# The last quarter of a seven-product matmul: one product moved to the end, cut into two column halves, and its last sums on VectorE

## The chip, the cores and the metric

One core of one Trainium2 chip runs the whole kernel. The metric is device time in microseconds (us), the median of several executions. Engines: TensorE (PE), VectorE (DVE), ScalarE (ACT), GpSimd (POOL) and SyncE (SP), which here only issues DMAs and waits.

## The reference, cut to what matters

```python
# x [8, 8, 512, 64], state [8, 8, 32, 64]; w_in [512, 2048], w_out [2048, 512]
a      = softmax(x @ state^T / 8)          # tokens read the states
xread  = a @ state
a2     = softmax(state @ x^T / 8)          # states read the tokens
sread  = a2 @ x
x      = concat([xread, sread], axis=2)    # 544 rows a batch, heads side by side: 4352 x 512
h      = x @ w_in
g      = max(h, 0) + alpha * min(h, 0)
out    = g @ w_out                         # float32, 4352 x 512
```

## The kernel before

**Blocks.** The 4352 rows are worked as nine blocks: block `b` from 0 to 7 holds the 512 token rows of batch `b`, block 8 all 256 state rows. In a block, `F` makes one of sixteen tiles of h (128 of the 2048 inner columns by all rows) in PSUM, `N` takes its negative part on ACT, `G` adds it back, scaled, on DVE: that is g, in float16. Four tiles of g make a group; `g_half(b, th, f)` is one half `th` of the rows of group `f`.

**The second matmul in seven products.** For blocks 1 to 8, g (row halves by inner halves) times w_out (inner halves by column halves) is done as a two-by-two product in seven products instead of eight. The sums of w_out that this needs are made once (`W`). The sums of g are made for each block: token `U.b.i.c.e` makes sum `i` (1 to 4) of inner quarter `c` on engine `e` (`p` is GpSimd, `v` VectorE); sum 2 needs sum 1, and sum 4 needs sum 2. Token `P.b.p.i.c` is product `p`, row part `i` of a half (two of them, in block 8 only one), inner quarter `c`: four matmuls of 256 columns that use four tiles of g, or of a sum, as weights (products 1, 2 and 4 use g itself, 5 sum 1, 6 sum 2, 7 sum 3, 3 sum 4). Line 736 is the one matmul of all products.

**Three accumulators.** In each block, PSUM bank x takes products 1, 6, 5 and 3 one after the other; after 1, after 6 and after 5 its content is copied aside by ACT (`K.b.1`, `K.b.2`, `K.b.4`, line 752). Bank y takes product 2 alone, bank v first 7 and then 4. Token `Q.b.th.dh` writes a quarter (row half `th`, column half `dh`) of the block: `Q.b.0.0` is y plus copy 1, `Q.b.1.1` is v after product 7 plus copy 4, `Q.b.1.0` is v after product 4 plus copy 2 (DVE, line 769), `Q.b.0.1` is x as it is after product 3 (a copy, line 767). SP then stores the quarter (line 770): 256 KB in blocks 1 to 7, 128 KB in block 8. So `Q.b.1.1` has to read v before product 4 is added to it, and each copy of x has to be done before the next product is added.

**Order and buffers.** The order is written out: a list of tokens, worked from left to right. Each engine's instructions stand in the order of the list, and an instruction waits until what it reads has been written, and until the buffer that it writes has been read by all that read the tile in it before. The buffers that matter here:

```python
osb = moe.tile([128, n_i, d_h], F32, name=f"oq_{b}_{th}_{dh}", tag="osb", bufs=4)
t = gss[b, i, c] = moe.tile(
    [128, 4, w], F16, name=f"gsum_{b}_{i}_{c}", tag=f"gsum{i}{c}", bufs=1
)
```

A quarter to be stored lies in one of four `osb` buffers and frees it when its store has landed; each sum of g has one buffer for all blocks, and frees it when the last matmul of its product is done. The list before ends (`g` of block 8 is done at its start):

```
G.8.9 P.7.5.1.0 U.8.3.0.p P.7.2.1.1 P.7.5.0.0 P.7.7.0.1 Q.7.0.0 P.7.7.1.1 P.8.2.0.1.1 K.7.4.a P.7.3.1.1 P.7.3.0.1
U.8.1.1.p U.8.2.1.p P.8.1.0.0.3 U.8.1.0.p U.8.2.0.p Q.7.1.1 P.7.4.0.1 P.7.4.1.0 P.8.1.0.1 K.8.1.a U.8.4.1.p P.7.4.0.0
P.7.4.1.1 Q.7.1.0 P.8.6.0.1 P.8.6.0.0 P.7.3.1.0 P.8.2.0.0 P.7.3.0.0 K.8.2.a P.8.5.0.1 U.8.3.1.p Q.8.0.0 P.8.5.0.0
K.8.4.a P.8.7.0.0.4 P.8.7.0.1 Q.7.0.1.v P.8.3.0.1 U.8.4.0.p Q.8.1.1 P.8.3.0.0 P.8.4.0.1 Q.8.0.1.a P.8.4.0.0 Q.8.1.0
```

At the very end SP waits, one after the other, for the semaphores of the DMAs and the engines (line 816), and then all engines meet in a barrier.

Of the kernel before, what the change touches and what calls it, by code (L numbers as in the profile page):

```python
# [8 lines left out]
F32 = mybir.dt.float32  # L9
# [29 lines left out]
tt.2 F.2.15.2 F.2.1.0 P.1.2.0.0 P.1.1.0.0 F.2.14.5 m.3.1 N.2.15 N.2.1 G.2.15 K.1.1.a N.2.14 mo.3.1.a G.2.1 G.2.14
m.3.0.1.2 mo.3.0.v.1 P.1.2.1.0 F.2.11.0 U.1.3.1.p mo.3.0.a.0 U.1.2.1.p P.1.6.1.1 N.2.11 F.2.2.5 N.2.2 F.2.0.2 N.2.0  # L40
U.1.1.0.p U.1.2.0.p U.1.4.0.p lx.4 P.1.6.0.1 Q.1.0.0 G.2.11 m.5.0.1.4 mo.5.0.a.0 G.2.2 mo.5.0.a.1 rd.2.0 rdo.2.a
G.2.0 sc.3 m.3.3.5.1 mo.3.3.a.1 tm.3 mo.3.3.v.0 m.4.0.4.2 mo.4.0.a.1 sb.3 P.1.6.1.0 P.1.6.0.0 xd.4 F.2.13.0 F.2.7.1
mo.4.0.a.0 F.2.8.2 K.1.2.a P.1.5.1.0 N.2.7 nb.3.a G.2.7 N.2.13 G.2.13 N.2.8 G.2.8 F.2.9.5 N.2.9 G.2.9 te.3.0
P.1.5.0.0 smax.3 P.1.7.1.1.4 F.2.10.1 N.2.10 F.2.5.0 N.2.5 G.2.5 G.2.10 F.2.4.2 N.2.4 G.2.4 te.3.1 P.1.5.1.1
U.1.3.0.p P.1.7.1.0 P.1.5.0.1 K.1.4.a U.1.4.1.p F.2.3.5 N.2.3 G.2.3 P.1.7.0.1 F.2.6.0 N.2.6 ssh.p.3 lx.5 F.2.12.1
N.2.12 G.2.6 P.1.7.0.0 P.1.3.1.0 m.6.0 Q.1.1.1 m.4.1.2.5 sexp.3 P.1.3.1.1 mo.6.0.a G.2.12 mo.4.1.a.0 ssum.3.0
U.2.1.0.p snorm.v.3 P.1.3.0.0 P.1.4.0.0 mo.4.1.a.1 P.1.3.0.1 U.2.2.0.p Q.1.0.1.a P.1.4.1.1 tsum.3 m.6.1.1.2 wb.3
mo.6.1.a.0 m.4.3 mo.4.3.a m.5.3.5.3 P.1.4.0.1 mo.5.3.a.1 P.2.1.0.1.1 P.2.1.1.0 P.1.4.1.0 mo.5.3.a.0 sc.4 U.2.1.1.p
U.2.2.1.p Q.1.1.0 U.2.4.1.p tn.3.0.p U.2.3.0.p U.2.3.1.p tm.4 mo.6.1.a.1 m.4.2.0.3 mo.4.2.a.0 F.3.15.5 xd.5 N.3.15
G.3.15 F.3.1.2 F.3.8.4 N.3.1 G.3.1 N.3.8 mo.4.2.a.1 P.2.1.0.0 F.3.12.0 N.3.12 G.3.8 nb.4.a P.2.1.1.1 F.3.7.5 G.3.12  # L50
# [52 lines left out]
def kernel(  # L103
# [38 lines left out]
    def single(k, name, shape, dtype):  # L142
        return ps.tile(shape, dtype, name=name, tag=f"k{k}", bufs=1)
# [584 lines left out]
    def product(b, p, i, c, k=None):  # L728
# [6 lines left out]
        for j in range(4):  # L735
# [85 lines left out]
```

## Time and profile before

| what | value |
|---|---|
| device time, median of 3 runs | 209.06 us (209.02, 209.06, 209.43) |
| span of the profiled execution, first to last instruction | 207.1 us |
| TensorE busy | 200.4 us, 97% of the span |
| GpSimd busy | 179.5 us, 87% |
| VectorE busy | 171.7 us, 83% |
| ScalarE busy | 155.3 us, 75% |
| moved by DMA | 23.68 MB, mean 114 GB/s |
| granted TensorE clock, mean | 0.996 |

Of the profiled execution only the span is given as its own time; the median of the runs is 2.0 us above that span, which is what lies around the first and the last instruction. Engine times are sums of busy time, and an engine that waits is not busy. The views give starts in us from the start of the span. A matmul's duration holds its way through the array, so several overlap: the pace of a stream of matmuls is read from the starts of neighbouring groups.

### The profile page before, as it was taken

The page shows a single profiled execution, that of the slowest core. Times are in us where ns is not written, and L with a number is a line of the kernel's source. Part 1 is how long each engine was busy: PE and PEld are TensorE (multiplying, and loading weights), DVE is VectorE, ACT ScalarE, POOL GpSimd, SP SyncE. Part 2 cuts the span into 40 slices and gives each one's busy share as a digit, 9 for nine tenths or more (in the row PEclk, how much of TensorE's full clock was granted, in tenths as well). Part 3 has the DMA queues.
Part 4 walks back from the last instruction along what each step waited for, and adds up shares of the span by engine and source line. Part 5 has one row for each costly group of instructions (what it writes and reads, how often), then busy time and mean ns, then how long its engine had stood idle before and what let it go on. Part 6 is the DMA issues. An engine that isn't in the chain of part 4 may idle for free.

```text
span 207.1 us, 5034 instructions
## 1 busy us (share of the span) xinstructions
PE 200.4 (97%) x1997; PEld 133.6 (65%) x1997; DVE 171.7 (83%) x251; ACT 155.3 (75%) x306; POOL 179.5 (87%) x113
## 2 busy tenths in 40 slices
PE   7899999999999999999999999999999999999992
PEld 2553344445566656687667856776877687788882
DVE  0889899999999999999999999999987967733231
ACT  4699999998999999997899787968755757502120
POOL 8177789997998999997997999797997999999960
PEclk9999999999999999999999999999999999999998
DMA  6999996698928798238976530126101200023223
GB/s 175 215 207 205 204 204 97 158 173 106 178 82 101 116 192 156 53 38 167 243 118 104 148 105 0 54 103 152 55 0 53 102 0 3 0 101 104 101 77 125
DMA packets 44038, 23.68 MB, mean 114 GB/s; under 512 B 22256, under 2 KB 43504, under 8 KB 44016
## 3 DMA queue, kind: packets, MB, share of 16 engines
q1 hardware_dynamic: 31152, 14.82, 28.4%
q0 software_dynamic: 11792, 8.09, 27.3%
q10 hardware_dynamic: 1072, 0.46, 0.9%
q8 instruction: 15, 0.25, 0.4%
q14 instruction: 7, 0.06, 0.1%
HBM read 17.31 MB, written 8.91 MB: 127 GB/s over the span
## 4 chain that ended last, share of the span: by engine, by line
PE 86%; DVE 5%; ACT 4%; DMA 2%; issue 1%; ACTq 0%
PE px L736 26%; PE h L577 24%; PE pv L736 13%; PE py L736 7%; PE m_ps L528 4%; PE h L586 3%; PE o L647 3%; DVE g L633 3%; DMA x<-in_x_dram 2%; PE sr_ps L501 2%; PE fill L253 2%; ACT neg L630 1%; PE sc L335 1%; ACT m L554 1%; PE xT_ps L320 1%
## 5 line engine op out<-in xcount | busy, mean ns | idle before, releaser
L633 DVE SCALAR_TENSOR_TENSOR g<-neg,oma_sb,h 128x512 f16<-128x512 f32 (+1 forms) x142 | 94.0, 711 | 11.6 <-ACT neg L630 11.0
L630 ACT ACTIVATE neg<-h 128x512 f32<-128x512 f32 (+1 forms) x142 | 75.6, 580 | 16.5 <-PE h L577 11.5
L577 PE MATMUL h<-aT,m 128*128 128x512 f16 x252 | 66.8, 380 | 0.1
L736 PEld LDWEIGHTS <-gsum 128*128 128x128 f16 x480 | 46.5, 98 | 13.1 <-issue 0.9
L736 PEld LDWEIGHTS <-g 128*128 128x128 f16 x360 | 34.7, 98 | 8.8 <-issue 1.4
L715 POOL TENSOR_TENSOR gsum<-g,g 128x1024 f16<-128x1024 f16 (+1 forms) x16 | 32.1, 2007 | 6.7 <-DVE g L633 4.9
L577 PEld LDWEIGHTS <-m 128*128 128x128 f16 x252 | 23.8, 98 | 18.4 <-issue 2.0
L715 POOL TENSOR_TENSOR gsum<-g,gsum 128x1024 f16<-128x1024 f16 (+1 forms) x16 | 32.0, 2005 | 1.5 <-PE px L736 1.0
L715 POOL TENSOR_TENSOR gsum<-gsum,g 128x1024 f16<-128x1024 f16 (+1 forms) x16 | 32.1, 2007 | 1.0
L736 PE MATMUL px<-ws,gsum 128*128 128x256 f16 x240 | 32.1, 273 | 0.0
L715 POOL TENSOR_TENSOR gsum<-g 128x1024 f16<-128x1024 f16 (+1 forms) x16 | 31.9, 2006 | 0.0
L752 ACT COPY kept<-px 128x512 f32<-128x512 f32 (+1 forms) x24 | 13.6, 567 | 21.0 <-PE px L736 20.9
L554 ACT CAST m<-m_ps 128x512 f16<-128x512 f32 x35 | 19.1, 602 | 1.5 <-PE m_ps L528 1.1
L769 DVE TENSOR_TENSOR oq<-pv,kept 128x512 f32<-128x512 f32 (+1 forms) x16 | 10.4, 649 | 10.6 <-PE pv L736 10.4
L736 PE MATMUL px<-w_out_sb,gsum 128*128 128x256 f16 x120 | 17.2, 273 | 0.0
L736 PE MATMUL px<-w_out_sb,g 128*128 128x256 f16 x120 | 17.2, 273 | 0.0
L405 POOL TENSOR_TENSOR ts<-ts,mx 128x1024 f32<-128x1024 f32 x7 | 13.3, 1911 | 4.4 <-DVE mx L400 4.4
L647 PE MATMUL o<-w_out_sb,g 128*128 128x512 f16 x64 | 16.6, 380 | 0.1
L736 PE MATMUL py<-w_out_sb,g 128*128 128x256 f16 x120 | 16.6, 273 | 0.0
L736 PE MATMUL pv<-ws,gsum 128*128 128x256 f16 x120 | 16.4, 273 | 0.0
L736 PE MATMUL pv<-ws,g 128*128 128x256 f16 x120 | 15.9, 273 | 0.0
L552 ACT CAST m<-m_ps 128x1024 f16<-128x1024 f32 x13 | 13.2, 1018 | 0.5 <-PE m_ps L528 0.4
(75 smaller groups left out, 238.1 us busy)
## 6 DMA issues: line engine op xcount, KB each, us to landing
out_dram<-oq SPq DMA_DIRECT2D x28, 256.0 KB, 2.6
xg<-in_x_dram POOLq DMA_DIRECT2D x7, 512.0 KB, 7.4
w_in_sb<-in_moe_w_in_dram POOLq DMA_DIRECT2D x4, 512.0 KB, 8.6
w_out_sb<-in_moe_w_out_dram POOLq DMA_DIRECT2D x4, 512.0 KB, 12.7
out_dram<-osb SPq DMA_DIRECT2D x4, 256.0 KB, 2.9
x<-in_x_dram SPq DMA_DIRECT2D x2, 256.0 KB, 3.7
out_dram<-oq SPq DMA_DIRECT2D x4, 128.0 KB, 2.1
x<-in_x_dram ACTq DMA_DIRECT2D x1, 256.0 KB, 4.6
```

Source lines behind the costliest of these rows:

```text
L405: engine(e).tensor_tensor(blocks(cols(live["ts", b], j, S)), blocks(scored(b, j)), over_blocks(cols(live["mx", b], j, S // N)), ALU.subtract,)
L528: nc.tensor.matmul(t[N * k : N * (k + 1), :], st_head(b, h)[64 * r : 64 * r + 64, :], w_in_sb[64 * r : 64 * r + 64, c, 512 * f : 512 * (f ...
L552: copier(e)(m_tile(b, f), t)
L554: copier(e)(m_tile(b, f)[:, g, :], t[g])
L577: nc.tensor.matmul(h.rearrange("p (r j s) -> p r j s", r=2, j=2), ms[b, f][:, g, 128 * j : 128 * (j + 1)], weights(b, g), start=(g == 0), ...
L630: nc.scalar.activation(neg, h, RELU, bias=0.0, scale=-1.0)
L633: nc.vector.scalar_tensor_tensor(g_tile(b, jc), negs.pop((b, jc)), oma_sb[:, jc : jc + 1], hs.pop((b, jc)), ALU.mult, ALU.add,)
L647: nc.tensor.matmul(outs[b, q], g_tile(b, jc)[:, 128 * q : 128 * (q + 1)], w_out_sb[:, jc, :], start=not begun and jc == 2 * jc2, stop=left ...
L715: engine(e).tensor_tensor(t, x(), y(), op)
L736: nc.tensor.matmul(pbanks[b, name][:, i, :], of(b, c)[:, j, 128 * i : 128 * (i + 1)], moving[:, 4 * c + j, :], start=not begun and j == 0, ...
L752: copier(e)(t, pbanks[b, "x"])
L769: nc.vector.tensor_tensor(osb, pbanks[b, name], kept[b, add], ALU.add)
```

## The change

- Product 2 of block 8 (`P.8.2.0.1` and `P.8.2.0.0`, eight matmuls of 256 columns) and `Q.8.0.0` are taken out of the middle of the list. In their place, at its end, `L.0` and `L.1` make the same product in two column halves of 128, each in a bank of its own (eight matmuls of 128 columns each), and `LO.0` and `LO.1` add copy 1 (DVE) and store 64 KB each, the first through ACT's queue, the second through SP's.
- Seven of the eight sums of g of block 8 are made on VectorE (`U.8.x.x.v`) and stand earlier in the list; `U.8.3.0` stays on GpSimd.
- `Q.7.0.1` stands a little earlier.
- The stores of `Q.3.1.1`, `Q.4.0.0` and `Q.4.1.1` are issued as two DMAs of 128 KB each.

```diff
 G.8.9 P.7.5.1.0 U.8.3.0.p P.7.2.1.1 P.7.5.0.0
+U.8.1.1.v U.8.2.1.v
 P.7.7.0.1 Q.7.0.0 P.7.7.1.1
-P.8.2.0.1.1
 K.7.4.a
+U.8.1.0.v U.8.2.0.v
 P.7.3.1.1 P.7.3.0.1
-U.8.1.1.p U.8.2.1.p
 P.8.1.0.0.3
-U.8.1.0.p U.8.2.0.p
 Q.7.1.1 P.7.4.0.1 P.7.4.1.0
+U.8.4.1.v U.8.3.1.v U.8.4.0.v
 P.8.1.0.1 K.8.1.a
-U.8.4.1.p
 P.7.4.0.0 P.7.4.1.1 Q.7.1.0 P.8.6.0.1 P.8.6.0.0 P.7.3.1.0
-P.8.2.0.0
 P.7.3.0.0 K.8.2.a P.8.5.0.1
-U.8.3.1.p Q.8.0.0
+Q.7.0.1.v
 P.8.5.0.0 K.8.4.a P.8.7.0.0.4 P.8.7.0.1
-Q.7.0.1.v
 P.8.3.0.1
-U.8.4.0.p
 Q.8.1.1 P.8.3.0.0 P.8.4.0.1 Q.8.0.1.a P.8.4.0.0
+L.0.1
 Q.8.1.0
+LO.0 L.1.0 LO.1
...
+    def last_part(n, k):
+        part = slice(d_h // 2 * n, d_h // 2 * (n + 1))
+        t = pbanks[B, "y", n] = single(k, f"py_{B}_{n}", [128, d_h // 2], F32)
+        for jc in range(n_h):
+            c, j = divmod(jc, 4)
+            nc.tensor.matmul(
+                t, g_half(B, 0, 2 + c)[:, j, :], w_halves[1, 0][:, jc, part],
+                start=(jc == 0), stop=(jc == n_h - 1),
+            )
+
+    def last_part_out(n):
+        part = slice(d_h // 2 * n, d_h // 2 * (n + 1))
+        osb = moe.tile([128, d_h // 2], F32, name=f"oq_{B}_0_0_{n}", tag="osb", bufs=4)
+        nc.vector.tensor_tensor(osb, pbanks[B, "y", n], kept[B, 1][:, 0, part], ALU.add)
+        (nc.sync if n else nc.scalar).dma_start(quarter_rows(B, 0, 0)[:, :, part], osb)
...
-        nc.sync.dma_start(quarter_rows(b, th, dh), osb if b < B else osb[:, 0, :])
+        to = quarter_rows(b, th, dh)
+        if b < B and e == 2:
+            for i in range(n_i):
+                nc.sync.dma_start(to[:, i, :], osb[:, i, :])
+        else:
+            nc.sync.dma_start(to, osb if b < B else osb[:, 0, :])
...
-        "W": w_sum, "U": g_sum, "P": product, "K": keep, "Q": quarter_out,
+        "W": w_sum, "U": g_sum, "P": product, "L": last_part, "LO": last_part_out, "K": keep, "Q": quarter_out,
```

(`Q.3.1.1`, `Q.4.0.0` and `Q.4.1.1` get a last argument of 2, which is `e` in the code above.)

More of the change, by code (lines that the diff above doesn't have):

```diff
@@ L96 @@
-K.8.1.a U.8.4.1.p P.7.4.0.0 P.7.4.1.1 Q.7.1.0 P.8.6.0.1 P.8.6.0.0 P.7.3.1.0 P.8.2.0.0 P.7.3.0.0 K.8.2.a P.8.5.0.1
-U.8.3.1.p Q.8.0.0 P.8.5.0.0 K.8.4.a P.8.7.0.0.4 P.8.7.0.1 Q.7.0.1.v P.8.3.0.1 U.8.4.0.p Q.8.1.1 P.8.3.0.0 P.8.4.0.1
-Q.8.0.1.a P.8.4.0.0 Q.8.1.0
+W.1.0.p G.0.6 S.0.1.0 m.1.1 F.0.10.1 N.0.4 G.0.4 mo.1.1.a N.0.10 G.0.10 F.0.8.3 S.0.1.3 S.0.1.2 ssh.p.1 sexp.1 F.0.9.0
+ssum.1.s N.0.9 lx.2 xd.2 S.0.0.3 N.0.8 G.0.8 F.0.11.1 N.0.11 S.0.3.3 W.1.1.p snorm.p.1 m.0.3 mo.0.3.a S.0.3.2 S.0.0.2
@@ new lines @@
+P.2.2.0.0 tsum.4 P.2.2.0.1 U.2.4.0.p lx.6 P.2.7.1.1 tm.5 P.2.7.0.1 F.3.5.2 F.3.13.4 sexp.4 G.3.10 nb.5.a te.5.0
+U.3.1.0.p U.3.2.0.p N.3.5 tn.4.0.a ssum.4.3 P.2.7.0.0 P.2.3.1.1 Q.2.1.1 P.2.2.1.1 snorm.v.4 P.2.3.0.1 te.5.1 G.3.5
+P.2.3.0.0 P.2.4.0.0 P.2.4.1.1 tsum.5 tn.4.1.a P.2.3.1.0 N.3.13 tn.5.1.a tn.5.0.a tt.5 wb.4 G.3.13 P.2.4.0.1
+P.3.1.0.0.3 P.2.4.1.0 Q.2.1.0 Q.2.0.1.a P.3.1.0.1 F.4.3.2 Q.2.0.0 F.4.7.4 N.4.3 F.4.11.1 U.3.1.1.p F.4.5.0 N.4.7
+P.3.1.1.1 G.4.3 F.4.10.5 G.4.7 N.4.11 G.4.11 F.4.9.2 F.4.12.4 P.3.1.1.0 F.4.8.1 N.4.5 G.4.5 N.4.10 G.4.10 U.3.2.1.p
@@ new lines @@
+N.4.9 G.4.9 F.4.2.0 K.3.1.a U.3.4.1.p N.4.12 G.4.12 P.3.6.0.0 N.4.8 F.4.13.5 G.4.8 N.4.2 G.4.2 P.3.6.1.0 N.4.13
+P.3.6.0.1 m.7.0.2.4 mo.7.0.a.0 mo.7.0.a.1 sb.5 rd.5.1 rdo.5.a tt.4 rd.4.0 rdo.4.a xd.6 G.4.13 F.4.14.2 N.4.14
+P.3.6.1.1 F.4.15.4 K.3.2.a sc.6 G.4.14 m.6.3.1.0 tm.6 m.7.3.5.2 N.4.15 P.3.5.1.1 G.4.15 mo.7.3.a.0 mo.7.3.a.1
+U.3.3.0.p mo.6.3.a.1 P.3.5.1.0 F.4.6.5 N.4.6 F.4.4.2 N.4.4 sb.6 G.4.4 P.3.5.0.1 smax.5 lx.7 P.3.5.0.0 P.3.7.0.0.4
+K.3.4.a nb.6.a te.6.0 F.4.0.0 N.4.0 U.3.3.1.p F.4.1.2 N.4.1 mo.6.3.a.0 P.3.3.0.1 te.6.1 P.3.7.1.0 U.3.4.0.p P.3.7.1.1
@@ new lines @@
+P.6.7.1.0 F.7.1.0 N.7.1 F.8.5.4 N.8.5 G.7.1 F.7.10.2 U.7.2.1.p N.7.10 G.7.10 P.6.5.0.0 K.6.4.a P.6.2.0.0.1 G.8.5
+F.7.9.0 P.6.2.1.1 P.7.1.0.1.2 P.7.1.0.0 N.7.9 P.6.2.0.1 G.7.9 P.6.2.1.0 P.6.7.0.0 F.8.9.4 P.6.3.0.1 P.7.2.0.0.0
+P.6.3.0.0 U.7.1.0.p Q.6.1.1 P.7.1.1.1 P.6.4.0.0 P.6.4.0.1 P.6.4.1.0 Q.6.0.0 P.6.4.1.1 Q.6.1.0 P.7.1.1.0 U.7.3.0.p
+P.6.3.1.0 F.8.7.1 P.6.3.1.1 P.7.2.1.0 U.7.2.0.p K.7.1.a P.7.6.1.1 P.7.6.0.0 N.8.7 G.8.7 P.7.7.0.0.5 P.7.6.0.1
+P.7.6.1.0 P.7.7.1.0 P.7.2.0.1 Q.6.0.1.v U.7.4.0.p K.7.2.a P.7.5.1.1 P.7.5.0.1 U.7.4.1.p N.8.9 G.8.9 P.7.5.1.0
@@ L99 @@
+U.8.3.0.p P.7.2.1.1 P.7.5.0.0 U.8.1.1.v U.8.2.1.v P.7.7.0.1 Q.7.0.0 P.7.7.1.1 K.7.4.a U.8.1.0.v U.8.2.0.v P.7.3.1.1
+P.7.3.0.1 P.8.1.0.0.3 Q.7.1.1 P.7.4.0.1 P.7.4.1.0 U.8.4.1.v U.8.3.1.v U.8.4.0.v P.8.1.0.1 K.8.1.a P.7.4.0.0 P.7.4.1.1
+Q.7.1.0 P.8.6.0.1 P.8.6.0.0 P.7.3.1.0 P.7.3.0.0 K.8.2.a P.8.5.0.1 Q.7.0.1.v P.8.5.0.0 K.8.4.a P.8.7.0.0.4 P.8.7.0.1
+P.8.3.0.1 Q.8.1.1 P.8.3.0.0 P.8.4.0.1 Q.8.0.1.a P.8.4.0.0 L.0.1 Q.8.1.0 LO.0 L.1.0 LO.1
 """
```

119 lines of the change are left out of this document (50 added, 69 removed).

## The prediction

> **What bounds the kernel now.** I read the page's busy times first, then the chain of waits at its end, then the timelines of the last 17 us, engine by engine.
>
> ```profile
> PE 200.4 (97%) x1997; PEld 133.6 (65%) x1997; DVE 171.7 (83%) x251; ACT 155.3 (75%) x306; POOL 179.5 (87%) x113
> ...
> PE 86%; DVE 5%; ACT 4%; DMA 2%; issue 1%; ACTq 0%
> ...
> 202.52 0.89 PE pv L736 x8
> 203.43 0.42 DVE oq L769
> ```
>
> TensorE is the bound, without a gap up to the end of its last matmul at 203.41. Time can therefore go in two places only: matmul time (or stalls) before that, or the tail behind it: one DVE sum, one store, SP's closing waits. The rows of the tail: the issue of the last store, the time to landing of that store, and the closing waits (nine, then the five that end last).
>
> ```profile
> 203.88 0.54 SPq L770 DMA_DIRECT2D out_dram<-oq  x1
> DMA to landing us min/median/max: 2.1/2.1/2.1
> L816 SPq EVENT_SEMAPHORE  x9: 28/28/28, 204.5 to 206.2; - x9
> ...
> L816 SPq EVENT_SEMAPHORE  x5: 28/28/28, 206.0 to 206.2; - x5
> ...
> out_dram<-oq SPq DMA_DIRECT2D x28, 256.0 KB, 2.6
> ...
> alpha_rows<-in_moe_alpha_dram SPq DMA_DIRECT2D x4, 2.0 KB, 4.4
> ```
>
> The store, issued at 203.88, lands 2.1 later, at about 205.96, and lets the fifth of nine waits pass at 206.0; the four behind it only tick by, to 206.2: 0.06 each, 0.24 in all, after which 0.9 of barrier follows. Why the fifth? The rows of the DMA view whose queue is SP's or ACT's (eleven, first and last shown) add up to 60 issues. My reading, which the nine waits fit but no row states: eight semaphores are taken in turn, a ninth wait in front is for GpSimd's queue; 60 = 7 x 8 + 4, so the last store has the fourth of eight, the fifth wait.
>
> **The sum is made against** the span of 207.1; the median of the runs is 209.06, 1.96 more, taken as unchanged.
>
> **The change, part by part.** *The moved product.* These rows give the pace of both forms, with the loading of weights (PEld):
>
> ```profile
> 193.62 0.60 PE L736 MATMUL py<-w_out_sb,g 128*128 128x256 f16 x4
> 194.06 1.04 PE L736 MATMUL px<-w_out_sb,gsum 128*128 128x256 f16 x8
> ...
> 195.37 0.38 PE L736 MATMUL pv<-ws,g 128*128 128x256 f16 x2
> ...
> 198.86 0.60 PE L736 MATMUL py<-w_out_sb,g 128*128 128x256 f16 x4
> 199.29 0.60 PE L736 MATMUL px<-w_out_sb,gsum 128*128 128x256 f16 x4
> ...
> 200.60 1.04 PE L736 MATMUL pv<-ws,gsum 128*128 128x256 f16 x8
> ...
> 202.35 1.04 PE L736 MATMUL pv<-ws,g 128*128 128x256 f16 x8
> ...
> 12.29 1.07 PE L320 MATMUL xT_ps<-ident,xg 128*128 128x128 f16 x16
> 13.19 0.39 PE L386 MATMUL at_ps<-ident,an 128*128 128x128 f16 x4
> ...
> L736 PEld LDWEIGHTS <-g 128*128 128x128 f16 x360 | 34.7, 98 | 8.8 <-issue 1.4
> ```
>
> Four matmuls of 256 columns take 0.44 (193.62 to 194.06), so taking out `P.8.2` saves 0.87. The new ones have 128 columns with full weights each; the nearest rows are the sixteen of line 320: (13.19 - 12.29)/16 = 0.056 each. Sixteen make 0.90: +0.03. Bounds: 0.056, and 0.098, the duration of one weight load, if none overlapped (+0.70). I take 0.056: same shape, and those weights overlapped. The Trainium skill ("TensorE: Matmul & The Clock Gate", Back-to-back issue gap) gives about 81 ns for a stream of weight load and 128-column matmul, by which this term would be +0.43; the rows of line 320 disagree, with 56.
>
> *The sums of g on VectorE.* No float16 sum runs on DVE in this trace. The nearest rows, by shape:
>
> ```profile
> L325 DVE COPY xT<-xT_ps 128x512 f16<-128x512 f16 x5 | 2.0, 409 | 0.1
> L769 DVE TENSOR_TENSOR oq<-py,kept 128x512 f32<-128x512 f32 x7 | 4.8, 681 | 1.2 <-PE py L736 1.2
> L769 DVE TENSOR_TENSOR oq<-pv,kept 128x256 f32<-128x256 f32 x2 | 0.8, 425 | 2.4 <-PE pv L736 2.4
> ...
> 190.56 1.47 PE L736 MATMUL px<-ws,gsum 128*128 128x256 f16 x12
> 192.51 0.69 DVE L769 TENSOR_TENSOR oq<-py,kept 128x512 f32<-128x512 f32 x1 [1.23 <-PE py L736]
> 193.00 0.59 ACT L752 COPY kept<-px 128x512 f32<-128x512 f32 x1 [2.24 <-PE px L736]
> ```
>
> A float16 copy of 512 takes 0.41, a float32 sum of 512 takes 0.68: these are the ends. I take 0.42, since all operands are float16 in runs of 128, as in the copy. GpSimd's time saved is worth nothing, no matmul waits for it. But four sums now stand on DVE ahead of `Q.7.1.1`, and `P.7.4.0.1` may not write bank v before that has read it. Taking out `P.8.2.0.1` brings `P.7.3.1.1` to 193.62, where ACT's copy (193.00 + 0.59, and 0.05 to release PE) holds it 0.02, and `P.7.4.0.1` from 195.37 to 194.95. DVE: sum 1 begins when `P.7.5.0.1` has read the buffer (eighth of the twelve at 190.56, over at 191.60): 191.64 to 192.06; sum 2 (0.05 for its own result) to 192.53; `Q.7.0.0` to 193.22; the other pair to 194.11; `Q.7.1.1` to 194.80, seen by PE at 194.85. It is in time by 0.10: no stall, while a sum takes under 0.445. The release of 0.05 is from these rows (21.84 + 1.01 = 22.85):
>
> ```profile
> 21.84 1.01 ACT L552 CAST m<-m_ps 128x1024 f16<-128x1024 f32 x1 [0.28 <-PE m_ps L528]
> ...
> 22.90 0.41 PE L528 MATMUL m_ps<-w_in_sb,stT 64*32 64x512 f16 x8 [0.17 <-ACT m L552]
> ```
>
> Behind that all of PE stands 0.85 earlier (0.87 less 0.02); product 4 has its place until 202.37, and the new 0.90 follow. ACT's copies have to keep up; the tightest is copy 2, as the matmuls between it and product 5 shrink from three groups to two:
>
> ```profile
> 198.67 0.37 ACT L752 COPY kept<-px 128x256 f32<-128x256 f32 x1 [1.38 <-PE px L736]
> ```
>
> It moves by 0.42 and ends at 198.62; `P.8.5.0.1` (199.73 before) starts at 198.88: 0.2 to spare.
>
> *A new wait on DVE.* `U.8.4.0` stands ahead of `P.7.3.0.0` in the list, but needs the buffer which that one reads last. DVE halts there until 199.29 + 0.60 - 0.85 = 199.04, and behind it wait `Q.7.1.0` and `Q.7.0.1`: sum 199.11 to 199.53, the two quarters (0.69 each) to 200.22 and 200.91, `Q.8.1.1` (its matmuls, 200.60 + 1.04 - 0.85, are over at 200.79) to 201.34, in time for `P.8.4.0.1` at 201.50. (`Q.7.0.1` is moved ahead on DVE past `Q.8.0.0` alone, which is gone.) No matmul waits, but the stores slip.
>
> *The four `osb` buffers.* The last three quarters need buffers freed by the landings of `Q.7.1.0`, `Q.7.0.1` and `Q.8.1.1`. Rows for issue pace and landing (the second landing is that of the 256 KB issued at 200.67):
>
> ```profile
> 200.00 0.57 SPq L770 DMA_DIRECT2D out_dram<-oq  x1
> 200.67 0.55 SPq L770 DMA_DIRECT2D out_dram<-oq  x1
> DMA to landing us min/median/max: 2.5/2.5/2.5
> ```
>
> `Q.7.1.0`: issued 200.25, lands 202.75 at the latest. `Q.7.0.1`: 200.94 to 203.44. `Q.8.1.1`: SP is free 0.10 after the issue before it, 201.59, lands 203.69. PE is done with `L.0` at 202.37 + 7 x 0.056 + 0.22 = 202.98 and with `L.1` at 203.43; so it is the landings that decide: `LO.0` from 203.49, `LO.1` from 203.78. A DVE sum of 128 columns is 0.29 (0.681, 0.425: 0.13 less per 128): to 204.07. Before, the last sum ended at 203.85: +0.22.
>
> *The last store.* 64 KB instead of 128. From 256 to 128 KB the landing falls from 2.5 to 2.1; half of that again would be 0.2, nothing is the other end; I take -0.17. ACT issues the store before it, behind its last copy and with nothing after it, so SP isn't held up; no store on that queue is in the trace, and 2.1 is taken as for SP's.
>
> *The split stores* raise the issues by three, and two stores for one make a fourth: 64 = 8 x 8. By the reading above the last store then has the last wait, and nothing ticks by behind it: -0.24. Their cost is 0.5 of SP each, in the middle:
>
> ```profile
> 136.52 0.53 SPq L770 DMA_DIRECT2D out_dram<-oq  x1
> ...
> 137.57 0.53 SPq L770 DMA_DIRECT2D out_dram<-oq  x1
> ...
> 140.20 1.33 SPq L486 DMA_TRANSPOSE e2T<-e  x1
> DMA to landing us min/median/max: 2.8/2.9/3.0
> ...
> 146.82 1.12 PE sr_ps L501 x64
> ```
>
> The tightest is the split at 136.52: the next issue moves by 0.15 and the transposes at 140.20 not at all. Even 1 us late, the second transpose (issued 141.7, landing 2.9 later) would be there before line 501 reads it at 146.82.
>
> Sum: +0.22 - 0.17 - 0.24 = -0.19: span 206.91, time 208.87.
>
> **The rivals.** A measurement of this kernel can tell about 0.2%, 0.42 us, from no change.
>
> *The buffers are free in time* (DVE gets through its quarters earlier, or stores land sooner than I took). `LO.1` then starts at 203.47 on PE's end and is over at 203.76: -0.09 - 0.17 - 0.24 = -0.50, 208.56. For it: my margin is only 0.3, and 2.5 to landing may be 0.1 too long. Against: two stores must both land earlier.
>
> *Slower: a float16 sum takes 0.68 on DVE.* `Q.7.1.1` then ends at 195.84, `P.7.4.0.1` starts 0.94 late, and `P.8.4.0.1` waits another 0.15 for `Q.8.1.1`. The buffers follow: `LO.1` ends at 205.27, +1.42 - 0.17 - 0.24 = +1.01, 210.07. It begins to cost at 0.445 a sum. For it: every DVE sum in the trace runs at that pace. Against: all of them have float32 operands.
>
> *DVE waits for GpSimd.* `U.8.1.1` would start only as `U.8.3.0` ends on GpSimd, 190.95 + 1.15 = 192.10, all DVE 0.46 later, PE 0.36: 209.23.
>
> ```profile
> 190.95 1.15 POOL L715 TENSOR_TENSOR gsum<-g 128x512 f16<-128x512 f16 x1
> ...
> 72.29 2.13 POOL L715 TENSOR_TENSOR gsum<-gsum,g 128x1024 f16<-128x1024 f16 x1
> ...
> 73.33 1.22 DVE L427 TENSOR_TENSOR an<-ts,r 128x1024 f16<-128x1024 f32 x1
> ```
>
> Against it: a DVE sum of two SBUF tensors began at 73.33, in the midst of a GpSimd sum, and neither was longer than its fellows. The Trainium skill ("SBUF — State Buffer", section "SBUF: two separate sides") has this rule, an exclusive lock on a shared pair of ports for the whole instruction; the rows at 72.29 and 73.33 disagree.
>
> *Weight loads set the pace*, 0.098 each: `L.1` ends at 204.06, `LO.1` at 204.39: +0.54 - 0.41 = +0.13, 209.19.
>
> *The turn of semaphores isn't as I read it*: 0.24 is not saved, 209.11.
>
> **How the numbers follow.** Forecast 0.52; buffers free 0.20; slow sums 0.11; lock 0.03; weight loads 0.06; semaphores 0.08. Faster by over 0.2% (below 208.64): most of the second and the low edge of the forecast, 0.22. Slower (above 209.48): slow sums and a little of the unforeseen, 0.14. Within: 0.64. The range goes from just below 208.56 to just above 209.23 and leaves out the slow sums: 208.5 to 209.3.
>
> **What would show it.** In the profile after: sixteen 128-column matmuls 0.056 apart; no gap of PE at `P.7.4.0.1`; DVE's sums near 0.42; DVE idle until about 199.1 ahead of `U.8.4.0`; the last two DVE sums waiting for a DMA, not for PE; the last closing wait right behind the last landing. A sum of 0.5 or more, or a PE gap near 195, makes it wrong; so does a last DVE sum that starts on PE's end.

## The result and the profile after

The changed kernel takes 210.75 us (median of 6 runs, 210.70 to 212.31) against 209.17 for the kernel before (208.92 to 209.43): 1.0100 times as long, 95% interval 1.0074 to 1.0125. The forecast was 208.87 and its range ended at 209.3, so it was wrong: the time rose by 1.6 where a fall of 0.2 was forecast. The profiled execution after took 210.71, with a span of 208.8.

The page of the kernel after, its span and busy times:

```profile
span 208.8 us, 5056 instructions
...
PE 200.8 (96%) x2005; PEld 134.0 (64%) x2005; DVE 174.5 (84%) x259; ACT 155.4 (74%) x306; POOL 171.8 (82%) x106
```

TensorE is busy for 0.4 longer and the span is 1.7 longer, so the time went into waiting. The view of waits of the kernel after, for the stretch from 195 to 206, says who waited for whom (us in total, times, longest):

```profile
DVE gsum L714 <- PE px L735: 3.5, 1, 3.5
ACT kept L767 <- DVE oq L784: 3.3, 1, 3.3
...
PE px L735 <- ACT kept L767: 1.6, 1, 1.6
```

This is a chain of three, and the timeline of the kernel after shows it (start, us, engine, line, out<-in; in brackets the idle time before it and what ended it). Line 714 is a sum of g, 784 and 782 write a quarter, 767 is the copy aside, 735 the matmul:

```profile
197.52 1.04 PE L735 MATMUL px<-ws,gsum 128*128 128x256 f16 x8
...
198.39 1.04 PE L735 MATMUL px<-w_out_sb,gsum 128*128 128x256 f16 x8
199.47 0.43 DVE L714 TENSOR_TENSOR gsum<-g,gsum 128x512 f16<-128x512 f16 x1 [3.51 <-PE px L735]
199.81 0.68 DVE L784 TENSOR_TENSOR oq<-pv,kept 128x512 f32<-128x512 f32 x1
200.41 0.68 DVE L782 COPY oq<-px 128x512 f32<-128x512 f32 x1
200.60 0.37 ACT L767 COPY kept<-px 128x256 f32<-128x256 f32 x1 [3.34 <-DVE oq L784]
201.03 1.03 PE L735 MATMUL px<-ws,gsum 128*128 128x256 f16 x8 [1.60 <-ACT kept L767]
```

Read from the bottom up. TensorE waited 1.60 us for ACT's copy 2 of block 8 (`K.8.2`) before `P.8.5.0.1`. ACT waited 3.34 us, and not for the bank that it copies, which was complete when the eight matmuls of 197.52 ended: it waited for DVE's `Q.7.1.0`. Copy 2 has one buffer for all blocks,

```python
t = kept[b, name] = moe.tile([128, n_i, d_h], F32, name=f"kept_{name}_{b}", tag=f"kept{name}", bufs=1)
```

and `Q.7.1.0` (v plus copy 2 of block 7) is the last that reads block 7's content. `Q.7.1.0` in turn stood on DVE behind `U.8.4.0`, which waited 3.51 us for `P.7.3.0.0`, since its own one buffer holds block 7's sum until then. Three instructions in a row, each right, and a late sum of g stops TensorE.

The tail of the kernel after, from the timeline, and the DMA view with the sizes of the last two stores:

```profile
204.52 1.06 PE L749 MATMUL py<-w_out_sb,g 128*128 128x128 f16 x16
...
205.16 0.29 DVE L757 TENSOR_TENSOR oq<-py,kept 128x128 f32<-128x128 f32 x1
...
205.69 0.29 DVE L757 TENSOR_TENSOR oq<-py,kept 128x128 f32<-128x128 f32 x1 [0.24 <-PE py L749]
```
```profile
out_dram<-oq ACTq DMA_DIRECT2D x1, 64.0 KB, 2.1
out_dram<-oq SPq DMA_DIRECT2D x1, 64.0 KB, 1.9
```

These lengths are as forecast, only later: sixteen matmuls of 128 columns, sums of 0.29, and 1.9 to the landing of the last store.

A note on comparing the traces: executions differ, mostly in the first 14 us, by 0.3 and now and then by 1.5, also with the kernel before; its profiled execution was an early one (span 207.1, where the median span of its later runs is 207.3 to 207.4). So the stages are compared below by what comes **after the start of the last instruction of g**, `G.8.9` on DVE. Its rows, before and then after:

```profile
190.80 0.48 DVE L633 SCALAR_TENSOR_TENSOR g<-neg,oma_sb,h 128x256 f16<-128x256 f32 x1 [2.40 <-ACT neg L630]
```
```profile
191.15 0.48 DVE L632 SCALAR_TENSOR_TENSOR g<-neg,oma_sb,h 128x256 f16<-128x256 f32 x1 [2.40 <-ACT neg L629]
```

From there to the start of the last instruction of the span, which takes 0.05 itself, the kernel before needs 16.26 and the kernel after 17.61, 1.35 more. "The tail" means this stretch from here on.

### The profile page after: what moved, and what is told of

Its sections match the earlier page's. It is cut to its first block, busy times and chain, and to the rows that moved or that the text cites. A ratio compares the mean times of both kernels' runs of the same rounds, so it can differ in the third digit from the quotient of the medians.

```text
span 208.8 us, 5056 instructions
## 1 busy us (share of the span) xinstructions
PE 200.8 (96%) x2005; PEld 134.0 (64%) x2005; DVE 174.5 (84%) x259; ACT 155.4 (74%) x306; POOL 171.8 (82%) x106
## 5 line engine op out<-in xcount | busy, mean ns | idle before, releaser
L735 PEld LDWEIGHTS <-g 128*128 128x128 f16 x352 | 34.0, 98 | 8.7 <-issue 1.4
L714 POOL TENSOR_TENSOR gsum<-g,g 128x1024 f16<-128x1024 f16 x14 | 29.8, 2129 | 6.7 <-DVE g L632 4.8
L714 POOL TENSOR_TENSOR gsum<-g 128x1024 f16<-128x1024 f16 (+1 forms) x15 | 30.8, 2065 | 0.0
L714 POOL TENSOR_TENSOR gsum<-gsum,g 128x1024 f16<-128x1024 f16 x14 | 29.8, 2130 | 0.9
L714 POOL TENSOR_TENSOR gsum<-g,gsum 128x1024 f16<-128x1024 f16 x14 | 29.7, 2126 | 0.5
L735 PE MATMUL py<-w_out_sb,g 128*128 128x256 f16 x112 | 15.4, 273 | 0.0
```

The lines of the kernel that those rows point to most:

```text
L714: engine(e).tensor_tensor(t, x(), y(), op)
L735: nc.tensor.matmul(pbanks[b, name][:, i, :], of(b, c)[:, j, 128 * i : 128 * (i + 1)], moving[:, 4 * c + j, :], start=not begun and j == 0, ...
```

## The experiments

**Theory A**: the 1.6 us stall comes from `U.8.4.0` standing ahead of `Q.7.1.0` on DVE, together with the one buffer of copy 2; nothing else in the change is dear. Rivals: sums of g on VectorE are slow in themselves or wait for GpSimd; or the product at the end costs the time. Three kernels break the chain at three different links.

**The sum behind the quarter.** One token moves:

```diff
-U.8.4.1.v U.8.3.1.v U.8.4.0.v P.8.1.0.1 K.8.1.a P.7.4.0.0 P.7.4.1.1 Q.7.1.0
+U.8.4.1.v U.8.3.1.v P.8.1.0.1 K.8.1.a P.7.4.0.0 P.7.4.1.1 Q.7.1.0 U.8.4.0.v
```

> Edit: in the list of the changed kernel U.8.4.0 stands right behind Q.7.1.0 instead of ahead of it. Theory A (DVE halts at U.8.4.0, so Q.7.1.0 is late, so copy 2 of block 8, which needs the one buffer that Q.7.1.0 reads, is late, so product 5 starts 1.6 to 1.8 us late): Q.7.1.0 runs near 197.5, PE has no gap ahead of product 5, and the time is 1.8 to 2.2 us under that of the changed kernel, 208.5 to 208.9, that is 0.3 to 0.6 under the kernel before. Rival B (the float16 sums on DVE cost the time: the first took 0.71 beside GpSimd, and bank v is freed late): nothing changes there, the time stays within 0.3 of the changed kernel, 210.4 to 211. Rival C (something at the start, where the trace after is 0.36 behind from 5 us on): the time falls only by what the gap was, to about 209.2, and stays level with before.

Measured: 208.92 (208.81 to 209.52), 0.9990 of before, interval 0.9977 to 1.0002. (The ratios here and below are not those of the two medians: executions that began 1.5 late, of either kernel, are in them too.) Tail 15.86 against 17.61: the one token is worth 1.75 us. The timeline of this kernel:

```profile
197.72 0.69 DVE L784 TENSOR_TENSOR oq<-pv,kept 128x512 f32<-128x512 f32 x1 [1.77 <-PE pv L735]
...
198.63 0.37 ACT L767 COPY kept<-px 128x256 f32<-128x256 f32 x1 [1.37 <-PE px L735]
199.26 1.04 PE L735 MATMUL px<-ws,gsum 128*128 128x256 f16 x8
```

The quarter runs 2.1 earlier, ACT now waits for the matmuls alone, and TensorE starts product 5 at 199.26 with no gap, 1.77 earlier than in the kernel after (201.03).

**Copy 2 in another buffer.** `U.8.4.0` stays where it halts DVE; only copy 2 of block 8 no longer shares the buffer that the halted quarter reads (the four buffers named `neg` are free once g of block 8 is done):

```diff
-        [128, n_i, d_h], F32, name=f"kept_{name}_{b}", tag=f"kept{name}", bufs=1
+        [128, n_i, d_h], F32, name=f"kept_{name}_{b}",
+        **(dict(tag="neg", bufs=4) if (b, name) == (B, 2) else dict(tag=f"kept{name}", bufs=1)),
```

> Edit: the changed kernel, with copy 2 of block 8 in a buffer of its own (one that the negative parts of h no longer need); U.8.4.0 stays ahead of Q.7.1.0, so DVE still halts until P.7.3.0.0 is done. Theory A: copy 2 runs near 198.9 although Q.7.1.0 still ends near 200.5, PE has no gap ahead of product 5, and what is left is the forecast's own case: the last two DVE sums wait for the landings of two stores, 208.8 to 209.1, level with before. If instead the halt of DVE holds PE by another way too (Q.8.1.1 ahead of product 4), a gap of some tenths stays there. Rival B: 210.4 to 211, the gap ahead of product 5 stays.

Measured: 209.81 (209.47 to 211.25), 1.0032 of before, 1.0012 to 1.0052, but the median span, 207.4, is that of before; the rest lies outside the span and comes back below. In the timeline of this kernel DVE halts just as long as in the kernel after, and TensorE doesn't notice:

```profile
199.13 1.04 PE L735 MATMUL px<-ws,gsum 128*128 128x256 f16 x8
199.33 0.42 DVE L714 TENSOR_TENSOR gsum<-g,gsum 128x512 f16<-128x512 f16 x1 [3.51 <-PE px L735]
199.67 0.68 DVE L785 TENSOR_TENSOR oq<-pv,kept 128x512 f32<-128x512 f32 x1
...
203.77 0.63 DVE L757 TENSOR_TENSOR oq<-py,kept 128x128 f32<-128x128 f32 x2 [0.31 <-PE py L749]
```

The halt of 3.51 does no harm to TensorE without the shared buffer. What is left is the case that the prediction worked out: the stores slip, and the last two sums wait for buffers that landings free. Those landings are at 203.64 and 203.98 in this trace, and the two sums start 0.12 behind them, at 203.77 and 204.11; the row's bracket names TensorE, but the matmuls of `L.0` were over at 203.23, and those of `L.1` at 203.68. Tail 16.20, 0.06 less than before.

**The sum in another buffer.** The same edit for `gsum` of `U.8.4.0` instead, copy 2 as it was.

> Edit: the changed kernel, with U.8.4.0 writing to a buffer of its own (one that the negative parts of h no longer need), at its place in the list. Theory A: U.8.4.0 doesn't wait for P.7.3.0.0 any more and runs near 196.0, Q.7.1.0 near 197.5, no gap ahead of product 5, last two sums on PE's end: 208.5 to 208.8, level with the kernel where U.8.4.0 stands behind Q.7.1.0. Rival B: the sums take what they took, so 210.4 to 211.

Measured: 208.85 (208.63 to 210.36), 0.9991, 0.9974 to 1.0007; tail 15.83, no gap of TensorE above 0.02. From the timeline of this kernel, the sum and then the quarter:

```profile
195.79 0.41 DVE L715 TENSOR_TENSOR gsum<-g,gsum 128x512 f16<-128x512 f16 x1
...
197.64 0.69 DVE L785 TENSOR_TENSOR oq<-pv,kept 128x512 f32<-128x512 f32 x1 [1.43 <-PE pv L736]
```

Breaking any one of the three links takes the stall away, so theory A is shown: the sum's one buffer, the order on DVE and the copy's one buffer are each necessary for the stall.

**The split stores alone.** Theory C (not the rival C above) is the prediction's reading of the closing waits: their number behind the last landing goes by the turn of the semaphores. The list of before, four stores split (64 issues), no product moved:

```diff
-... Q.3.1.1 ... Q.3.0.0 ... Q.4.0.0 ... Q.4.1.1 ...
+... Q.3.1.1.2 ... Q.3.0.0.2 ... Q.4.0.0.2 ... Q.4.1.1.2 ...
```

> Edit: the list of the kernel before, with four of its stores (Q.3.0.0, Q.3.1.1, Q.4.0.0, Q.4.1.1) issued as two DMAs each, nothing else: 64 issues on the queues of SP and ACT instead of 60. By the prediction's reading of the closing waits the last store then has the last of the nine: the four waits of 0.06 behind its landing are gone, 0.24 us, 208.9 where before is 209.17. If the turn of semaphores is not so, the waits behind the last landing stay five and the time is that of before. If the split stores cost anything in the middle, a gap of PE appears near 115 to 147 us.

Measured: 208.89 (208.81 to 209.31) against 209.12 for before on the same chip, 0.9984, 0.9966 to 1.0001. The median says -0.23, the interval touches no change, and the tail gives it more sharply: 16.00 against 16.26, nearly all of it behind the last landing (0.87 instead of 1.11).

**One split more.** As before it, with `Q.2.1.1` split too: 65 issues, so the last store should have the first semaphore, and more ticking follows.

> Before's order with five quarters' stores split (Q.2.1.1 joins the four of the run with four splits), so 65 stores and loads share eight semaphores in turn. Theory C (the closing waits go by the turn of the semaphores, first to last, 0.06 us each): the last store now has the first semaphore, so seven waits follow its landing: the last wait ends 7 x 0.06 = 0.42 us later than in the run with four splits, about 0.18 behind the kernel before, time about 209.3. Rival (the gain of the four splits came from shorter stores): no change against the run with four splits, 208.9, and at most one wait behind the last landing.

Measured: 209.28 (209.13 to 211.09), 1.0015, 0.9990 to 1.0039; tail 16.41, 0.41 more than with four splits (expected 0.42). The closing waits from the last landing on, in the kernel with four splits (window from 206.2, landing at 206.26) and in this one (window from 207.5, landing at 207.59; this execution began 1.3 late):

```profile
L836 SPq EVENT_SEMAPHORE  x1: 28/28/28, 206.3 to 206.3; - x1
```
```profile
L836 SPq EVENT_SEMAPHORE  x8: 27/28/28, 207.6 to 208.0; - x8
```

One wait against eight (the first of them is the landing's own), 0.4 us, with one issue more: 60, 64 and 65 issues leave four, none and seven waits behind the landing. In these traces the DMAs of SP and ACT go through eight semaphores in a fixed turn, and the last store has the fourth, the eighth and the first of them. The reading of the semaphores' turn is shown.

**The sums back on GpSimd.** The order of before, with the product at the end and the three splits; no sum on VectorE:

```diff
-U.8.1.1.v U.8.2.1.v P.7.7.0.1 Q.7.0.0 P.7.7.1.1 K.7.4.a U.8.1.0.v U.8.2.0.v P.7.3.1.1 P.7.3.0.1 P.8.1.0.0.3
-... U.8.4.1.v U.8.3.1.v U.8.4.0.v ...
+P.7.7.0.1 Q.7.0.0 P.7.7.1.1 K.7.4.a P.7.3.1.1 P.7.3.0.1 U.8.1.1.p U.8.2.1.p P.8.1.0.0.3 U.8.1.0.p U.8.2.0.p
+... U.8.4.1.p ... U.8.3.1.p ... U.8.4.0.p ...
```

> Edit: the list of the kernel before, with product 2 of block 8 at the end in two column halves and the three split stores, but all sums of g of block 8 on GpSimd where they stood. Theory A (the loss came from the sums in DVE's queue, above all U.8.4.0; the moved product by itself gains): no gap of PE above 0.03 near 195 or 200, Q.7.1.0 near 197.7, U.8.4.0 on GpSimd ends near 200.4, in time for P.8.3.0.0 near 201.4; span 207.0, time 208.8 to 208.9. Rival (GpSimd is too slow now that the product no longer stands between: product 6 or product 3 waits for its sums): gaps of 0.1 to 0.8 ahead of product 6 near 197.5 or product 3 near 201, time 209.0 to 209.6.

Measured: 208.88 (208.70 to 210.33), 0.9985, 0.9966 to 1.0003; tail 15.81: without the sums on VectorE nothing is lost. But the moved product itself gains little on TensorE. Of the 0.45 by which this tail is shorter than that of before, 0.26 lie behind the last landing (the turn of semaphores), 0.18 are the smaller last store, and the last sum ends only 0.02 earlier. GpSimd's last sum is over at 200.6 (started at 199.46, 1.15 long), and product 3 needs it at about 201.3.

**GpSimd's sum twice.** In the four traces so far with sums on VectorE, the first of them took 0.69 to 0.71, the others 0.41 to 0.43. Either it is slowed while GpSimd sums, or it is blocked until GpSimd is done. The kernel with the sum in another buffer, and `U.8.3.0` made twice in a row:

```diff
-U.8.3.0.p P.7.2.1.1
+U.8.3.0.p U.8.3.0.p P.7.2.1.1
```

> Edit: the changed kernel with U.8.4.0 in a buffer of its own, and the sum U.8.3.0 made twice in a row on GpSimd (the second time into the same buffer, with the same values), so that GpSimd is busy until about 193.6 instead of 192.4 while DVE makes its first sums. So far the first float16 sum on DVE took 0.69 to 0.71 and ended 0.28 behind the end of GpSimd's sum in four traces, the later ones 0.42. If a DVE sum of two SBUF operands is blocked until GpSimd's instruction is done: the first one still ends 0.28 behind the first GpSimd sum, near 192.7, or behind the second, near 193.9, and one of the first two takes over 0.9; Q.7.1.1 ends 0.7 later, P.7.4.0.1 starts 0.6 to 0.8 late, span 207.6 to 207.8. If a DVE sum only runs at half its pace while GpSimd is busy: the first two take about 0.70 each, Q.7.1.1 ends 0.28 later and PE 0.25, span 207.3. If the first sum is long for a reason of its own (its start, its operands): the second stays at 0.42 and the span at 207.0.

There is one execution alone, and it began 1.6 late: 211.23, tail 16.65 against 15.83. Its timeline (GpSimd's two sums from windows of their own):

```profile
192.84 1.16 POOL L715 TENSOR_TENSOR gsum<-g 128x512 f16<-128x512 f16 x1
...
193.57 0.71 DVE L715 TENSOR_TENSOR gsum<-g,g 128x512 f16<-128x512 f16 x1 [0.42 <-PE px L736]
...
194.08 1.22 POOL L715 TENSOR_TENSOR gsum<-g 128x512 f16<-128x512 f16 x1
...
194.39 1.19 DVE L715 TENSOR_TENSOR gsum<-gsum,g 128x512 f16<-128x512 f16 x1
...
197.62 1.03 PE L736 MATMUL pv<-ws,g 128*128 128x256 f16 x8 [0.64 <-DVE oq L785]
```

The second sum, begun in the midst of GpSimd's second, takes 1.19 and ends at 195.58, 0.28 behind the end of GpSimd (194.08 + 1.22 = 195.30); the first ended 0.28 behind the end of GpSimd's first (194.00). At half pace sums of these lengths would have ended at no fixed distance: it is a block until GpSimd is done. The Trainium skill ("SBUF — State Buffer", sections "SBUF: two separate sides" and "Who interferes with whom") says just this, an exclusive lock that a VectorE sum with both inputs in SBUF meets while GpSimd reads SBUF; here it holds. Its price was 0.8 us, as now `P.7.4.0.1` waits.

**No sum on GpSimd.** The kernel with the sum in another buffer, with `U.8.3.0` on VectorE too, behind `U.8.3.1`:

> Edit: the changed kernel with U.8.4.0 in a buffer of its own and U.8.3.0 on DVE behind U.8.3.1, so that GpSimd does nothing while DVE makes the sums of block 8. If GpSimd's sum was what made the first DVE sum long: it takes 0.41 to 0.43, Q.7.1.1 ends 0.28 earlier, the 0.02 to 0.04 that P.7.4.0.1 starts late is gone, and the time falls by that little: 208.8, not to be told from the kernel with the buffer alone (208.85). If the first sum is long for a reason of its own it stays at 0.70.

Measured: 209.03 (208.91 to 210.44), 1.0002, 0.9980 to 1.0024. The first sum's row in this kernel's timeline shows it gone from 0.71 to 0.43, and no wait at `P.7.4.0.1` is left:

```profile
191.97 0.43 DVE L715 TENSOR_TENSOR gsum<-g,g 128x512 f16<-128x512 f16 x1 [0.42 <-PE px L736]
```

The tail is 15.82 all the same: in the change the lock costs TensorE 0.04 at most, and at the end the landing that frees the last sum's buffer decides; it comes at 203.70, level with the last matmul.

**Nothing waits.** The kernel before this one, with the two parts of the last quarter in free buffers and `P.8.1.0.0` ahead of `P.7.3.1.1`, so that copy 4 has time:

```diff
-K.7.4.a U.8.1.0.v U.8.2.0.v P.7.3.1.1 P.7.3.0.1 P.8.1.0.0.3
+K.7.4.a U.8.1.0.v U.8.2.0.v P.8.1.0.0.3 P.7.3.1.1 P.7.3.0.1
...
-osb = moe.tile([128, d_h // 2], F32, name=f"oq_{B}_0_0_{n}", tag="osb", bufs=4)
+osb = moe.tile([128, d_h // 2], F32, name=f"oq_{B}_0_0_{n}", tag="neg", bufs=4)
```

> Edit: as the kernel with no sum of block 8 on GpSimd, and the two last parts lie in buffers that nothing else needs any more instead of the four osb buffers, and P.8.1.0.0 stands ahead of P.7.3.1.1, so that copy 4 of block 7 is done before its bank is written. This is meant as the best version. Theory: no wait of PE near 193.9 or 195.3 (0.05 saved), and the last DVE sum starts 0.04 to 0.05 behind PE's end instead of 0.12 (0.08 saved): span 206.85, time 208.7, 0.4 under before. If the wait in front of the last sum has another cause than the buffer, it stays at 0.12 and the time at 208.8.

Measured: 208.85 (208.61 to 210.44), 0.9981, 0.9954 to 1.0009; tail 15.75, 0.51 less than before, no wait of TensorE at all.

The same two edits on the kernel with the sums on GpSimd, the smallest change with nothing waiting (its expectation counts the tail to the end of the last instruction, about 0.05 more than here):

> The change without its move of sums to VectorE (as in the run that keeps them on GpSimd), and in addition: the two parts of the last quarter in buffers that are free, and P.8.1.0.0 ahead of P.7.3.1.1, so that copy 4 has more time. Theory: no wait of TensorE is left at all; from the last instruction of g to the end 15.78 us against 15.86 with the sums on GpSimd alone and 16.28 in the kernel before; span 206.9, time 208.7 to 208.8. Rival (the landings of the last stores set the end whatever TensorE does): 15.86 as before this edit, time 208.9. Whether the time shows it depends on what lies outside the span, which has been 1.8 to 2.4 for these builds.

Measured: 208.87 (208.73 to 210.06), 0.9992, 0.9977 to 1.0007; tail 15.74. In the timelines of the two kernels with the sums on GpSimd, without and with these edits, the last sum begins 0.12 and then 0.04 behind the end of the matmuls:

```profile
203.82 0.29 DVE L757 TENSOR_TENSOR oq<-py,kept 128x128 f32<-128x128 f32 x1 [0.23 <-PE py L749]
```
```profile
203.83 0.29 DVE L757 TENSOR_TENSOR oq<-py,kept 128x128 f32<-128x128 f32 x1 [0.15 <-PE py L749]
```

The tail lost 0.07 (15.81 to 15.74), the time nothing that can be told. Tails of 15.74 to 15.86, 0.4 to 0.5 less than before, should give times of 208.6 to 208.7; they give 208.85 to 209.03. The difference lies outside the span: the kernels with the product at the end spend 1.84 to 2.41 there (medians; 2.41 is copy 2 in another buffer, and its single executions go from 2.07 to 2.79), those without it, before and the two with splits alone, 1.78 to 1.80.

**Both last parts stored through SP.** The last two kernels test whether the store on ACT's queue is what is paid there: copy 2 in another buffer, and the smallest change, both with

```diff
-        (nc.sync if n else nc.scalar).dma_start(quarter_rows(B, 0, 0)[:, :, part], osb)
+        nc.sync.dma_start(quarter_rows(B, 0, 0)[:, :, part], osb)
```

> The run with copy 2 in a free buffer, and the first part of the last quarter stored through SP's queue instead of ACT's. Every kernel with L and LO has spent 1.84 to 2.41 us outside its span (this one 2.41), every kernel without them 1.78 to 1.80. Theory: it is the store on ACT's queue that is paid for there; without it the time outside the span goes back to 1.8. The price: SP issues one store more, so the last one is issued about 0.34 later, span 207.4 + 0.34 = 207.7, time 209.5 against 209.81. Rival (it is something else in these builds): outside 2.4 still, time 210.1.

> The run with sums on GpSimd and nothing waiting, and the first part of the last quarter stored through SP's queue instead of ACT's. Theory: outside the span 1.8 instead of 1.90; the last store is issued about 0.40 later behind the one before it on SP: span 207.0 + 0.4 = 207.4, time 209.2 against 208.87. Rival: outside 1.90 as before, time 209.3.

Measured: the first 209.47 (0.9995, 0.9970 to 1.0021), outside the span 1.78 instead of 2.41; the second 209.39 (0.9995, 0.9960 to 1.0030), outside 1.93 instead of 1.90. By their medians both are slower than before, by 0.32 and 0.24; late starts, which 5 of 18 executions of before had here, hide that in the ratios. The theory holds for the one and falls for the other; the store on ACT's queue is not the whole cause. That the second store on SP comes later was as expected in kind: tail +0.30 and +0.52, expected 0.34 and 0.40. What the 0.1 to 0.6 outside the span are stays open.

| kernel | time | tail | median span | outside |
|---|---|---|---|---|
| before | 209.12 to 209.17 | 16.26 | 207.3 to 207.4 | 1.79 |
| after | 210.75 | 17.61 | 208.8 | 1.91 |
| the sum behind the quarter | 208.92 | 15.86 | 207.0 | 1.86 |
| copy 2 in another buffer | 209.81 | 16.20 | 207.4 | 2.41 |
| the sum in another buffer | 208.85 | 15.83 | 207.0 | 1.84 |
| split stores alone, four | 208.89 | 16.00 | 207.1 | 1.79 |
| split stores alone, five | 209.28 | 16.41 | 207.4 | 1.80 |
| sums on GpSimd | 208.88 | 15.81 | 207.0 | 1.92 |
| no sum on GpSimd | 209.03 | 15.82 | 207.0 | 2.06 |
| nothing waits | 208.85 | 15.75 | 207.0 | 1.91 |
| sums on GpSimd, nothing waits | 208.87 | 15.74 | 207.0 | 1.90 |
| copy 2 in another buffer, both parts through SP | 209.47 | 16.50 | 207.7 | 1.78 |
| sums on GpSimd, nothing waits, both parts through SP | 209.39 | 16.26 | 207.4 | 1.93 |

No version is faster than before beyond doubt: the better medians are 0.20 to 0.32 lower, with intervals that end just above 1.

## Why the prediction was wrong

**The step that failed** is the last sentence of "A new wait on DVE": "No matmul waits, but the stores slip." Up to it the step was right to a few hundredths. Shifted by the 0.36 by which `G.8.9` is later in this trace, DVE starts `U.8.4.0` at 199.11 (forecast 199.11) and `Q.7.1.0` at 199.45 (199.53). But the step asked what stood behind the halted instruction on its own engine, followed the stores, and checked of TensorE only `P.8.4.0.1`. It didn't ask who waits for the **buffers that those instructions read**. The paragraph on ACT's copies, just above, made the same mistake from the other end: it moved copy 2 by 0.42 because its matmuls end earlier, to 198.62, and "0.2 to spare"; the copy's other condition, its one buffer free of block 7, wasn't looked at. In the profile before it had never shown: the copy's row at 198.67 waits for TensorE alone. The copy began 1.99 later than forecast (200.60 less 0.36, against 198.25), and product 5 1.79 later (201.03 less 0.36, against 198.88). With the halt and without the shared buffer, the tail is 0.06 below that of before; with both, it is 1.35 above.

**The miss as a sum.** In the profiled executions: forecast 208.87, after 210.71. The span ended 17.66 behind the start of `G.8.9` (the tail of 17.61 and the 0.05 of the last instruction), and 16.11 was forecast (span 206.91 less 190.80): 1.55. `G.8.9` itself was 0.36 later than in the profile that the sum was made against, which had begun early. Outside the span 1.90, taken as 1.96. Together that is the miss of 1.84, but for 0.01 of rounding.

**The terms that the runs bear out.** *The moved product*: sixteen matmuls in 1.06, of which the last takes 0.22: (1.06 - 0.22)/15 = 0.056 apart, as taken from the transposes of line 320. The 81 ns of the Trainium skill ("TensorE: Matmul & The Clock Gate", Back-to-back issue gap) don't hold for this stream, and the rival of weight loads falls. *Sums on VectorE*: 0.41 to 0.43, forecast 0.42; the rival of 0.68 falls. *The last store*: with 64 KB the last sum's end is 1.92 ahead of the landing instead of 2.09, -0.17 as forecast. *The turn of semaphores*: -0.24 forecast; 0.25 less behind the landing in the kernel after (0.86 against 1.11), and 0.24 with the splits alone. *The split stores*: the issue behind the one at 136.52 was to move by 0.15 and didn't move at all (137.93 less 0.36, against 137.57).

*The `osb` buffers*: +0.22 forecast for the end of the last sum. In the kernel that has this case, copy 2 in another buffer, it is +0.31 against `G.8.9`, of which 0.05 are TensorE's: right in kind, 0.09 too small. Its whole tail came to -0.06 instead of -0.19: 0.09 of the gap is this term, 0.05 the landing, 1.97 behind the last sum there.

**The rivals.** *Buffers free in time* (208.56) is what the kernel with nothing waiting became, tail -0.51 where -0.50 was worked out; its time is 208.85, as 0.13 more than in before lies outside the span. *DVE waits for GpSimd* had its mechanism argued away, and wrongly. The counter-row, line 427 at 73.33, was misread as a sum of two SBUF tensors. It is a product, and every such product on VectorE belongs to a batch from 2 to 7 (those of batches 0 and 1 run on GpSimd), for which the second operand `r1` is a tile of `single` (the first branch below is that of batch 1),

```python
if jk == "s":
    live["r1", b] = att.tile([128, 2 * S // N], F32, name=f"r1_{b}", tag="r1", bufs=2)
elif b:
    live["r1", b] = single(jk, f"r1_{b}", [128, 2 * S // N], F32)
```

and that lies in PSUM. So the row had one input in SBUF and, unlike the prediction says, it doesn't disagree with a rule on two. The lock was there, in the kernel after as in the others: its first sum on VectorE and GpSimd's,

```profile
191.33 1.16 POOL L714 TENSOR_TENSOR gsum<-g 128x512 f16<-128x512 f16 x1
192.05 0.71 DVE L714 TENSOR_TENSOR gsum<-g,g 128x512 f16<-128x512 f16 x1 [0.42 <-PE px L735]
```

It made that sum 0.29 longer. But DVE's instructions overlap a little (in this kernel the quarter at 193.21 starts 0.34 behind a sum of 0.42), so `Q.7.1.1` ended only 0.13 later than worked out; with the margin of 0.10 that left TensorE a wait of 0.04 at `P.7.4.0.1`, where 0.36 was priced. So it decided nothing, but the chance of 0.03 rested on a wrong reading. *No rival* had the chain that came: a halt on one engine that holds the buffer of another's copy.

**What would show it.** Four of the six signs came as written: the matmuls' pace, the sums (but for the first), DVE idle until 199.1, and the last closing wait right behind the last landing. "No gap of PE at `P.7.4.0.1`" was off by 0.04, and of the last two sums only the last came behind a landing (205.57), level with the end of the matmuls. By its own signs of being wrong, a sum of 0.5 or more and a gap near 195, the prediction had failed too: a sum of 0.71 and the 0.04. But neither was what cost the time. All signs looked at places where a wait had been thought of; a sign for TensorE as a whole, no gap from 190 to the end, would have named the failure.

## What to carry to other kernels

Where an instruction is moved ahead and has to wait, list everything behind it on its engine, and for each the tiles that it reads as well as those that it writes: with one buffer, the next writer of what it reads waits too, on another engine, and its reader after it. A single-buffered tile has two conditions, its data and its last reader; check both whenever either moves. And before a row is used against a rule, look up in the code in which memory each operand lies.

## What the hardware showed that was not expected

- A float16 sum on VectorE with both inputs in SBUF that started during a GpSimd sum of SBUF tensors ended 0.28 behind GpSimd's end: it took 0.69 to 0.71 and 1.19 instead of 0.42. The row shows no wait, only a longer instruction.
- Eight DMA semaphores, taken in turn, set how many closing waits of 0.06 follow the last landing: none, four and seven here, so up to 0.4 us, by the mere number of DMAs in the kernel.
- All kernels with the product at the end but one spend 0.05 to 0.6 us more outside the span (medians) than those without; one store moved to another queue took 0.63 of it away in one kernel and nothing in another. The cause is open.
